# Adding two accumulators of exponentials: by a VectorE instruction, or by an accumulating transfer that GpSimd issues

## The chip, the cores and the metric

One Trainium2 chip; the program runs on one of its cores. The metric is the device time of the whole kernel in microseconds, median over runs. The trace calls the engines PE (TensorE matmul), PEld (TensorE weight load), DVE (VectorE), ACT (ScalarE), POOL (GpSimd) and SP (SyncE, which issues most transfers). Shapes are partitions x elements.

## The reference

Two layers, one after the other. The first is attention with 4 batches, 8 heads, 768 positions and head size 64, in which a query sees the keys that fall into the same of 16 clusters. The second mixes tokens and channels.

```python
def _attn_ref(q, k, v, centroids):
    ...
    mask = q_assign[:, :, :, None] == k_assign[:, :, None, :]
    scores = scale * np.matmul(q, k.transpose(0, 1, 3, 2))
    scores = np.where(mask, scores, -1000000000.0)
    scores = scores - np.max(scores, axis=-1, keepdims=True)
    attn = np.exp(scores)
    attn = attn / (np.sum(attn, axis=-1, keepdims=True) + 1e-09)
    return np.matmul(attn, v).astype(np.float32)

def _moe_ref(x, w_theta, w_tok_r, w_tok_i, w_ch):
    theta = x @ w_theta
    zr, zi = x * np.cos(theta), x * np.sin(theta)
    y = np.einsum('ts,bsd->btd', w_tok_r, zr) + np.einsum('ts,bsd->btd', w_tok_i, zi)
    u = x + y
    return (u + np.maximum(u @ w_ch, 0.0)).astype(np.float32)
```

The change touches the row sums of `attn` alone, the denominator.

## The kernel before

**Pairs, halves, units.** The attention works on 16 pairs of heads (4 batches x 4 pairs; `pi` is the pair, `j` the head in it). The queries of a pair stand in two halves of 384 (`a` = 0, 1), the keys in six blocks of 128 (`i`). A half and a block of keys make a unit, so a pair has 12 units, numbered through (`u` = 12 `pi` + 6 `a` + `i`). The loop goes two units at a time, 192 units in all.

**A unit.** TensorE makes the scores of the key block against the half, transposed, keys on the partitions, once for each head (line 374, tile `sc`). ScalarE takes exp into `at`, a tile of 128 x 768 for both heads (line 437). TensorE multiplies `at` with the values (line 509, `av`). Ten units ahead TensorE also makes the scores with queries on the partitions (line 374, tile `m`), of which VectorE takes the maximum (line 396, `nm`).

**The sums.** The sum over keys is a sum over six units and then over 128 partitions. GpSimd adds the `at` of units 0 to 2 of a half into one accumulator, `acc[a, 0]`, those of units 3 to 5 into another, `acc[a, 1]` (`add_exps`, line 448, two additions each; `TERMS` = 3). `add_sums` then adds the second to the first (line 452). `sums` lets TensorE add over the partitions with a column of ones (line 476, `sm`), one product for each head and half, ScalarE adds a small constant (line 482, `se`), and the sums go out through DRAM, come back spread over partitions, are inverted (line 494, `sq`) and come back broadcast (line 499, `rb`). `normalise` multiplies the pair's output with them (line 530, `xt`; on GpSimd for pairs 0 to 13, on VectorE for the last two) and stores it (line 533). In the last pair `add_sums` isn't called; TensorE adds both accumulators there.

**The order.** It is written out by hand. `at_unit(u, fn, ...)` puts a function on the list of a unit, and the loop takes the lists up as it comes to the units, in order of unit and, on one unit, in the order in which they were put there. At the end of each step `in_order` chains the instructions of each engine, those that issue transfers too, in the order in which they were written. What bears on the change:

```python
        if pi < NPAIR - 1:
            for a in range(2):
                at_unit(7 if pi == a == 0 else u + ADDS[a], add_sums, pi, a)
        stages([u + NU + k for k in SUMS], sums(pi))
        stages([u + NU + k for k in NORM], normalise(pi))
```

This stands in the loop over pairs, with `u` = 12 `pi`, `NU` = 12, `ADDS` = (8, 13), `SUMS` = (4, 6, 8, 9, 10) and `NORM` = (13, 16). So, counted in units from the start of a pair: the first half's accumulators are added at unit 8, the second half's at 13, and TensorE sums over the partitions at 16. On unit 13 also stands `normalise` of the pair before, put on the list one turn of the loop earlier. Within a step the loop writes the scores of unit `u` and `add_exps(u)`, then the lists up to `u`, then scores, exp and `add_exps(u + 1)`, then the list of `u + 1`.

**Buffers.** `acc` has six buffers, taken in turn, four by each pair. `at` has six.

**The rest.** Beside the units GpSimd makes the low parts of queries and keys (line 360), and in the first ten pairs those of weights (line 159). VectorE converts weights from 64-bit floats (lines 137 to 146) and finds the clusters (lines 278 to 286, 339). After the attention comes the second layer (lines 729 to 941), with a first rotation of it (line 550) laid into the last units.

Of the kernel before, what the change touches and what calls it, by code (L numbers as in the profile page):

```python
# [14 lines left out]
ALU = mybir.AluOpType  # L15
# [26 lines left out]
def kernel(  # L42
# [19 lines left out]
    nc = tc.nc  # L62
# [386 lines left out]

    def add_sums(pi, a):  # L450
        s = st[pi]
        nc.vector.tensor_tensor(out=s["acc", a, 0], in0=s["acc", a, 0], in1=s["acc", a, 1], op=ALU.add)  # L452

    def both(products, u, then, *banks):
        interleave(*(products(u, j, *banks) for j in range(2)))
# [213 lines left out]
    for pi in range(NPAIR):  # L669
        u = NU * pi  # L670
        if pi > 0:
            prepare(pi, g1 if pi == 1 else assign(pi))
            at_unit(u - NU + 7, load_v, pi)
        for a in range(2):
            at_unit(u + a * NT - LEAD + NT, shift_row, pi, a)
# [5 lines that stand above are left out]
# [312 lines left out]
```

## Time and profile before

| what | before |
|---|---|
| median of 3 runs | 800.63 us (800.31 to 800.96) |
| span of the profiled execution | 798.5 us, mean granted TensorE clock 0.996 |
| time of the profiled execution itself | not given beside the span |
| DMA | 67.13 MB, mean 84 GB/s |
| transfers issued by GpSimd | none |
| additions of line 452 | 30 (two for each of 15 pairs) |

The profile is one execution, its times counted from the first instruction. A group's row has the line, the engine, the operation, what it writes and reads, and how often; then busy time, the mean of one, and the idle time before it with what ended it. The chain of work that ended last is followed back from the last instruction: at each step to what released it. Matmuls are pipelined and their ends are modelled, so TensorE shown busy need not be at its peak. The attention takes up to about 455 us, the second layer the rest.

### The profile page before, as it was taken

The numbers are of one execution on the slowest core, as the hardware profiler recorded it, in microseconds if no ns is written. First come the engines' busy times: TensorE is split into PE (matmuls) and PEld (weight loads), VectorE is DVE, ScalarE is ACT, GpSimd is POOL, SyncE is SP. The second block draws the span as 40 slices with busy tenths as digits, with TensorE's granted clock in tenths as the row PEclk, the third lists the DMA queues.
The fourth block names the chain that finished last, engine by engine and source line by source line (L and its number), as shares of the span: only waits on it lengthen the run. The fifth ranks groups of instructions, "written<-read, shape, count | busy, mean of one in ns | idle before, by whom it ended". The sixth has DMA issues, their size and how long they took to land.

```text
span 798.5 us, 14338 instructions
## 1 busy us (share of the span) xinstructions
PE 783.2 (98%) x5634; PEld 582.6 (73%) x5634; DVE 555.6 (70%) x664; ACT 399.9 (50%) x801; POOL 491.6 (62%) x284
## 2 busy tenths in 40 slices
PE   6999999999999999999999899999999999999998
PEld 5666656565656666666665588898889988899998
DVE  5789999999999999999888669543234433532322
ACT  3366666766767676666655546432433233504310
POOL 3388888999999999888978324551225112322131
PEclk9899999999999999999999999999999999999999
DMA  3232324332443244433452343003000400020001
GB/s 118 60 97 77 104 77 150 103 130 74 147 132 110 79 134 152 131 111 121 124 185 75 114 135 136 1 36 124 0 1 1 158 1 1 1 80 1 1 21 60
DMA packets 30894, 67.13 MB, mean 84 GB/s; under 512 B 8900, under 2 KB 14636, under 8 KB 30444
## 3 DMA queue, kind: packets, MB, share of 16 engines
q1 hardware_dynamic: 30540, 65.80, 25.1%
q8 instruction: 44, 0.72, 0.4%
q10 hardware_dynamic: 288, 0.43, 0.1%
q14 instruction: 22, 0.18, 0.1%
HBM read 50.79 MB, written 15.32 MB: 83 GB/s over the span
## 4 chain that ended last, share of the span: by engine, by line
PE 91%; DVE 6%; issue 1%; DMA 1%; ACT 1%; SPq 0%; ACTq 0%; DVEq 0%
PE y L862 25%; PE sc L374 24%; PE av L509 15%; PE tp L594 8%; PE cy L885 5%; PE m L374 3%; PE cp L885 3%; PE sm L476 2%; PE lg L263 2%; PE xp L587 1%; DVE nm L396 1%; PE y L885 1%; DVE acc L452 1%; PE lt L275 1%; DVE w L146 1%
## 5 line engine op out<-in xcount | busy, mean ns | idle before, releaser
L437 ACT ACTIVATE at<-sc 128x384 f32<-128x384 f32 x384 | 173.4, 493 | 96.6 <-PE m L374 59.7
L396 DVE TENSOR_REDUCE nm<-m 128x1 f32<-128x768 f32 x192 | 179.6, 945 | 21.4 <-PE m L374 17.1
L448 POOL TENSOR_TENSOR acc<-at,at 128x768 f32<-128x768 f32 x64 | 129.3, 2021 | 36.9 <-ACT at L437 36.5
L374 PE MATMUL m<-hk,hq 64*128 64x384 f32 x384 | 146.9, 387 | 0.9 <-DVE nm L396 0.8
L509 PE MATMUL av<-at,vt 128*64 128x384 f32 x768 | 145.7, 499 | 0.4 <-ACT xt L524 0.2
L816 POOL TENSOR_TENSOR zlc<-ab,zhc 128x512 fp32r<-128x512 f32 x24 | 32.2, 1340 | 177.3 <-ACT zhc L814 177.3
L448 POOL TENSOR_TENSOR acc<-acc,at 128x768 f32<-128x768 f32 x64 | 132.5, 2070 | 10.0 <-ACT at L437 7.9
L374 PE MATMUL m<-mk,mq 64*128 64x384 f32 x384 | 127.9, 337 | 0.8 <-DVE mk L303 0.8
L374 PE MATMUL sc<-hq,hk 64*128 64x384 f32 x384 | 117.7, 390 | 0.5 <-ACT at L437 0.5
L374 PEld LDWEIGHTS sc<-hq,hk 64*128 64x128 f32 x384 | 56.1, 184 | 61.9 <-issue 28.2
L374 PE MATMUL sc<-lq,hk 64*128 64x384 f32 x384 | 98.1, 336 | 0.0
L374 PE MATMUL sc<-mq,mk 64*128 64x384 f32 x384 | 97.8, 334 | 0.0
L374 PE MATMUL sc<-hq,lk 64*128 64x384 f32 x384 | 97.6, 334 | 0.0
L509 PEld LDWEIGHTS av<-at,vt 128*64 128x64 f32 x768 | 46.7, 136 | 59.4 <-issue 53.4
L599 DVE TENSOR_SCALAR kk<-tp 128x512 int32<-128x512 f32 x23 | 15.9, 690 | 95.1 <-PE tp L594 95.1
L374 PEld LDWEIGHTS m<-hk,hq 64*128 64x128 f32 x384 | 70.7, 185 | 3.5 <-DVE nm L396 2.7
L374 PEld LDWEIGHTS m<-mk,mq 64*128 64x128 f32 x384 | 71.4, 187 | 1.0 <-ACT hq L356 1.0
L452 DVE TENSOR_TENSOR acc<-acc,acc 128x768 f32<-128x768 f32 x30 | 70.6, 2352 | 0.0
L876 POOL TENSOR_TENSOR ul<-xT,uh 128x384 fp32r<-128x384 f32 (+1 forms) x36 | 33.8, 962 | 40.6 <-ACT uh L875 35.9
L588 ACT COPY xn<-xp 128x512 f32<-128x512 f32 x23 | 13.5, 586 | 84.2 <-PE xp L587 84.2
L374 PEld LDWEIGHTS sc<-mq,mk 64*128 64x128 f32 x384 | 55.2, 185 | 0.0
L374 PEld LDWEIGHTS sc<-lq,hk 64*128 64x128 f32 x384 | 55.2, 186 | 0.0
(173 smaller groups left out, 1735.5 us busy)
## 6 DMA issues: line engine op xcount, KB each, us to landing
rawq<-in_qT_dram SPq DMA_DIRECT2D x16, 384.0 KB
vt<-in_v_dram SPq DMA_DIRECT2D x16, 384.0 KB
rb<-sd SPq DMA_DIRECT2D x32, 192.0 KB
xT_d<-xt SPq DMA_DIRECT2D x16, 384.0 KB
rawk<-in_kT_dram SPq DMA_DIRECT2D x15, 384.0 KB
w<-in_wrT_dram SPq DMA_DIRECT2D x6, 768.0 KB
w<-in_wiT_dram SPq DMA_DIRECT2D x6, 768.0 KB
xT<-xT_d SPq DMA_DIRECT2D x3, 1536.0 KB
```

What stands on the lines that cost most here:

```text
L263: nc.tensor.matmul(lg[32 * g:32 * g + 32], lhsT=cb[:, p, :, :], rhs=raws[n][:, a * HS:(a + 1) * HS], start=True, stop=True)
L374: nc.tensor.matmul(out, lhsT=stat[r, cols], rhs=mov[r, over], start=start, stop=stop)
L396: nc.vector.tensor_reduce(out=s["nm", a][:, j, i // 2:i // 2 + 1], in_=s["m", j][:, :, 0:HS], op=ALU.max, axis=AX.XY, negate=True)
L437: last_exp[0] = nc.scalar.activation(out=s["at", a, i][:, j], in_=s["sc", j], func=AF.Exp, scale=SCALE)
L448: last_acc[0] = nc.gpsimd.tensor_tensor(out=s["acc", a, x], in0=prev, in1=at, op=ALU.add)
L452: nc.vector.tensor_tensor(out=s["acc", a, 0], in0=s["acc", a, 0], in1=s["acc", a, 1], op=ALU.add)
L509: nc.tensor.matmul(s["av"][64 * j:64 * j + 64], lhsT=s["vt"][:, i, j, :], rhs=s["at", a, i][:, j], start=(i == 0), stop=(i == NT - 1))
L594: nc.tensor.matmul(tp, lhsT=xx[:, c, :], rhs=w_th[c][k], start=(n == 0), stop=(n == 3 * NCT - 1))
L816: nc.gpsimd.tensor_tensor(out=zl, in0=tr, in1=zh.bitcast(F32), op=ALU.subtract)
L862: nc.tensor.matmul(y_at(b, d, c0, c1), lhsT=zz[:, d * P:(d + 1) * P], rhs=ww[:, c0:c1], start=first and lead, stop=last, skip_group_check= ...
L876: nc.gpsimd.tensor_tensor(out=ul[:, d, :], in0=x, in1=uh[:, d, :].bitcast(F32), op=ALU.subtract)
L885: nc.tensor.matmul(cp, lhsT=w_c[d][k][:, e * P:(e + 1) * P], rhs=uu[:, d, :], start=(n == 0), stop=(n == 3 * NCT - 1), skip_group_check=True)
```

## The change

`add_sums` calls GpSimd's transfer instead of VectorE's addition: `acc[a, 1]` is the source, `acc[a, 0]` the destination, both in SBUF, and the DMA engines add the source to what the destination holds. The place on the units' lists is the same.

```diff
     def add_sums(pi, a):
         s = st[pi]
-        nc.vector.tensor_tensor(out=s["acc", a, 0], in0=s["acc", a, 0], in1=s["acc", a, 1], op=ALU.add)
+        nc.gpsimd.dma_start(out=s["acc", a, 0], in_=s["acc", a, 1], accum_op=ALU.add)
```

## The prediction

> **What bounds the kernel now.** I read first the page's busy times and slices, then its chain of work by engine.
>
> ```profile
> span 798.5 us, 14338 instructions
> ...
> PE 783.2 (98%) x5634; PEld 582.6 (73%) x5634; DVE 555.6 (70%) x664; ACT 399.9 (50%) x801; POOL 491.6 (62%) x284
> ...
> PE   6999999999999999999999899999999999999998
> ...
> DVE  5789999999999999999888669543234433532322
> ...
> POOL 3388888999999999888978324551225112322131
> ...
> PE 91%; DVE 6%; issue 1%; DMA 1%; ACT 1%; SPq 0%; ACTq 0%; DVEq 0%
> ```
>
> TensorE carries 91% of the chain, VectorE 6%. In the attention, up to about 455 us, VectorE and GpSimd are nearly as full as TensorE. So an addition taken from VectorE is worth only what of that 6% it causes, and one engine that is almost as full receives something. How evenly TensorE runs there is read from the chain in order of time: the same product, one step of the loop, starts once per pair of heads.
>
> ```profile
> 84.30 1.44 PE av L509 x8
> ...
> 104.02 2.51 DVE acc L452
> ...
> 110.81 1.44 PE av L509 x8
> ...
> 130.52 2.51 DVE acc L452
> ...
> 137.31 1.44 PE av L509 x8
> ...
> 163.27 1.44 PE av L509 x8
> ...
> 262.66 1.44 PE av L509 x8
> ...
> 288.59 1.44 PE av L509 x8
> ...
> 423.28 2.28 DVE acc L452
> ```
>
> A pair takes 26.51 and 26.50 us where the addition stands on the chain (pairs 2 and 3), 25.96 in the next and 25.93 in the middle. The addition is on the chain three times of 30. Everywhere else TensorE paces the pair and VectorE's load is covered by it.
>
> **What goes from VectorE.** The view of line 452, and of two GpSimd lines beside it (ns, least/median/most):
>
> ```profile
> L452 DVE TENSOR_TENSOR acc<-acc,acc x30: 949/2306/2594, 48.3 to 423.3; 128x768 f32<-128x768 f32 x30
> ...
> who waited for it (us, times):
> ...
> L530 POOL TENSOR_TENSOR xt<-xt,rb x14: 1846/2558/2562, 89.0 to 424.7; 128x768 f32<-128x768 f32 x14
> ```
>
> Thirty additions go; the group sums to about 30 x 2.3 = 69 us of VectorE. One took 0.95 us, the median 2.31: most of that is waiting beside GpSimd's own additions. Nobody is listed as waiting for them. Their worth in time: pairs 2 and 3 fall to the 25.96 of pair 4, 2 x 0.54 = 1.1 us. The third place on the chain is the end of the attention:
>
> ```profile
> 437.48 2.08 DMA sq<-sd
> ...
> 439.72 0.64 DVE kk L599
> ...
> 438.27 1.07 PE L594 MATMUL xp_tp<-wth_hi,xl 128*128 128x512 f32 x4
> ```
>
> There VectorE's 2.28 us would move the transfer of sq forward, but the next instruction, kk, also needs the product that ends at 439.34. So kk can move by 0.4 us of the 2.3, and I take 0.4 (ends 0 and 2.3). If TensorE were not the cover in the other pairs, the additions would be worth up to 27 x 0.95 us; the even 25.93 us says it is.
>
> **Where the transfer stands.** One pair in the timeline (start, duration; order of the engines as written):
>
> ```profile
> 259.87 2.59 DVE L452 TENSOR_TENSOR acc<-acc,acc 128x768 f32<-128x768 f32 x1
> ...
> 261.72 2.42 POOL L448 TENSOR_TENSOR acc<-acc,at 128x768 f32<-128x768 f32 x1
> ...
> 270.04 1.83 POOL L448 TENSOR_TENSOR acc<-at,at 128x768 f32<-128x768 f32 x1 [0.42 <-DMA rb<-sd]
> ...
> 270.38 2.31 DVE L452 TENSOR_TENSOR acc<-acc,acc 128x768 f32<-128x768 f32 x1
> ...
> 271.83 2.56 POOL L530 TENSOR_TENSOR xt<-xt,rb 128x768 f32<-128x768 f32 x1
> ...
> 276.55 0.16 PEld L476 LDWEIGHTS sm<-acc,ecol 128*32 128x32 f32 x8 [0.60 <-issue]
> ```
>
> The first half's sum (259.87) is wanted by sm at 276.55, 16.7 us later: any transfer is hidden there. The second half's sum is not so free. VectorE has it ready at 272.69, 3.9 us ahead of sm. GpSimd comes to it late: unit 13's work list holds the multiplication of the pair before (L530) ahead of the sum, and GpSimd issues in that order. So the transfer leaves after unit 13's addition, which ends at 271.87, and after L530, which without VectorE beside it takes 1.85 (its least): 273.72. That leaves **2.8 us** until TensorE reaches sm. Behind sm in TensorE's queue stand the scores and maxima of the next units, so a late sum stops ScalarE and VectorE too; and as TensorE paces the pair, each microsecond late is a microsecond of the kernel, once per pair. VectorE's and SP's queues lose and gain no wait. The six buffers of the accumulators stand it: the buffer that the transfer reads is next written 14 units later for the first half and 15 for the second.
>
> **What the transfer takes.** The profile of before has no transfer issued by GpSimd and none that adds, so I bound it. The nearest rows: a lone store of 384 KB (the same bytes) with the DMA share around it, and the start of the kernel, where two reads of 384 KB run together. The rows of numbers are stretches: from and to, length, busy us of TensorE, its weight loads, VectorE, ScalarE and GpSimd, then clock, DMA share and GB/s.
>
> ```profile
> 410.71 0.33 SPq L156 DMA_DIRECT2D wd5r<-w  x1
> ...
> 410.60:411.40 0.80, 0.80 (x12) 0.60 (x10) 0.80 (x2) 0.80 (x3) 0.34 (x1) 1.00 0.00 0
> 411.40:412.80 1.40, 1.40 (x14) 0.77 (x12) 0.87 (x2) 1.19 (x3) 1.40 (x1) 1.00 0.79 285
> 412.80:414.00 1.20, 1.20 (x10) 0.50 (x7) 1.10 (x2) 0.26 (x1) 1.12 (x2) 1.00 0.00 0
> ...
> 0.72 3.48 DMA rawq<-in_qT_dram
> ...
> rawk<-in_kT_dram ACTq DMA_DIRECT2D x1, 384.0 KB
> ...
> L221 POOL TENSOR_TENSOR cs<-cs,half 128x1 f32<-128x1 f32 x1 | 0.6, 572 | 2.1 <-DVE cs L218 2.1
> ```
>
> - Low end: the store is done by 412.80, 2.1 us after its issue began. It moves the bytes once and SP issued it.
> - Like for like in bytes read: an accumulating transfer reads source and destination, 2 x 384 KB. That is what rawq and rawk read together, and rawq landed 3.48 us after its issue.
> - GpSimd's own time to issue: between SP's 0.33 and a whole pass over the tile, 1.83; its smallest arithmetic instruction took 0.57. I take the middle, 1.08.
>
> My value: 3.48 - 0.33 + 1.08 = **4.2 us**; low end 2.1; high end 1.83 + 3.15 + one more pass of data (3.48 - 2.08, the small transfer above against the large) = 6.4. I take the middle because two reads and a different issuer both lengthen the lone store, and nothing here shows a second pass. The stall is then 4.2 - 2.8 = **1.4 us per pair**, between 0 and 3.6.
>
> The Trainium skill, DMA: Bandwidth & Descriptors, Anatomy of one DMA, gives another sum: for transfers issued from GpSimd about 2.0 us and the bytes at 436 GB/s, an estimate of 2.9 us for these 393,216 bytes, hence a stall of 0.1 and a time near 801. No run here shows such a transfer. Against it the skill's Collectives: The Full Stack, The bandwidth ceiling, says that an adding transfer runs at half the rate of a copying one because it reads two sources; that would add 0.9 us by the same figure, an estimate of 3.8 and a stall of 1.0.
>
> **GpSimd's budget.** In the same pair:
>
> ```profile
> 262.66:288.59 25.93, 25.93 (x216) 15.85 (x218) 24.56 (x25) 17.55 (x38) 25.36 (x13) 1.00 0.36 118
> ```
>
> GpSimd is busy 25.36 of 25.93 us. It gets back what VectorE's additions cost it: L530 goes from 2.56 to 1.85, and the addition at 261.72 from 2.42 to the 1.83 of an undisturbed one, 1.3 us together. It pays two issues, 2.2. New load 26.2, in a pair that the stall makes 27.3 long: it fits, so I add nothing; if it didn't, unit 13 would start late and the difference would add to the stall. The DMA engines are 0.36 busy; two more transfers of some 2.5 us each leave them well below full.
>
> **The last two pairs** have less room:
>
> ```profile
> 401.22 1.85 POOL L530 TENSOR_TENSOR xt<-xt,rb 128x768 f32<-128x768 f32 x1 [1.00 <-DMA rb<-sd]
> ...
> 404.80 0.53 PE L476 MATMUL sm<-acc,ecol 128*32 128x384 f32 x4
> ...
> 422.94 1.81 POOL L448 TENSOR_TENSOR acc<-at,at 128x768 f32<-128x768 f32 x1 [2.00 <-ACT at L437]
> ...
> 427.99 0.85 PE L476 MATMUL sm<-acc,ecol 128*32 128x384 f32 x8
> ```
>
> Pair 13: 404.80 - 403.07 = 1.7, stall 2.5. Pair 14: 427.99 - (424.75 + 1.85) = 1.4, stall 2.8. Pair 0 has no L530 ahead of its sum (L530 runs 14 times on GpSimd, for pairs 1 to 14), so nothing for it.
>
> **Sum.** 12 x 1.4 + 2.5 + 2.8 = 22.1; less 1.1 and 0.4: +20.6 us. The page gives the span, 798.5, 2.1 under the median of 800.63, and no time of the profiled execution itself; I work in differences and add them to the median: **821 us**. With the high end: 12 x 3.6 + 4.7 + 5.0 - 1.5 = +51, 852. With the low end: 0.4 + 0.7 - 1.5 = -0.4, 800.
>
> **Rivals.**
> - *The transfer is hidden (not slower).* It lands within 2.8 us of L530's end; that is the point from which it decides. For it: the lone store took 2.1 us and in these microseconds no large transfer runs. Against: the second read and GpSimd's issue. Time: 800.63 - 1.5 = 799.1 if the last pairs hide too, 800.2 if they don't. The skill's fit named above falls here.
> - *GpSimd becomes the bound (slower).* Its load is 24.1 us and two issues; a pair lasts 25.9 plus the stall, which also grows with one issue. It decides from an issue of about 2.2 us, above my upper bound of 1.83. With 2.5 a pair takes 29.1, 3.2 more, 14 times: 844.
> - *The adding is slow in the DMA engines (slower still).* Landing 8 us after L530: 5.2 per pair, 12 x 5.2 + 13 - 1.5 = +74, 874. No row speaks for it; none excludes it.
>
> **How the numbers follow.** A change of 0.2%, 1.6 us, is about what this kernel's measurement can tell. My forecast (a stall of 0.3 to 3.6 us per pair) 0.62; hidden 0.20; GpSimd bound 0.08; slow adding 0.10. All but the hidden case are slower: 0.80. The hidden case gains 0.4 to 1.5 us, which is just short of 0.2%: same 0.15, faster 0.05 for a tail that gives more than 0.4. The range starts below the hidden case, 799.5, and ends at 848, near the high end; it leaves out most of slow adding and a part of the gainers, under 2 in 10. The forecast's own range is 803 to 852.
>
> **What would show it.** VectorE's busy time near 486 us. Line 452 on GpSimd, 30 issues of about 1.1 us. L530 and the additions behind it near 1.85. Ahead of sm, TensorE idle 1.4 us per pair on a wait for the transfer into acc, and the steps of the middle pairs 27.3 us apart, those of pairs 2 and 3 too. Were the pairs 25.9 us apart, the transfer was hidden; were GpSimd without idle time at unit 13, it is the bound. The prediction fails if GpSimd's issue together with the landing is under 2.8 us or over 6.4.

## The result, and the profile after

The changed kernel takes 913.33 us (median of four runs, 911.14 to 920.16), the kernel before 800.80 beside it: a ratio of 1.1415, 95% interval 1.137 to 1.1459, 112.5 us more. The profiled execution took 911.14 us, its span is 909.3. The page's busy times, three of its rows of slices, the queue of GpSimd's transfers, the chain by engine and the median landing of the transfers:

```profile
span 909.3 us, 14373 instructions
...
PE 831.6 (91%) x5634; PEld 603.0 (66%) x5634; DVE 586.9 (65%) x634; ACT 401.7 (44%) x801; POOL 471.7 (52%) x314
...
PE   7998898798799798798789878999999999999998
...
DVE  5877887888888898887896635685333433343222
...
POOL 3585686686687685675675653265222512241231
...
q0 software_dynamic: 4320, 11.80, 7.3%
...
PE 74%; issue 11%; DVE 9%; DMA 5%; ACT 1%; SPq 1%; POOL 0%; POOLq 0%; ACTq 0%; DVEq 0%
...
acc<-acc POOLq DMA_DIRECT2D x30, 384.0 KB, 4.7
```

GpSimd has less work than before (471.7 us, was 491.6) and gaps in every slice of the attention: it is not the bound. TensorE carries 74% of the chain instead of 91%, and its busy time rose by 48 us for the same 5634 products, so they take longer in the records. VectorE lost thirty additions and yet is busy 31 us longer. The three lines that matter: GpSimd's transfer, a step of the weight conversion on VectorE, and the multiplication that was expected to get faster (ns, least/median/most).

```profile
L452 POOL DMA_DIRECT2D acc<-acc x30: 851/868/1056, 49.4 to 530.5; - x30
...
DMA to landing us min/median/max: 3.9/4.7/6.3
...
L140 DVE TENSOR_SCALAR w<-w x16: 550/8934/9750, 40.2 to 527.3; 128x768 int32<-128x768 int32 x12, 128x512 int32<-128x512 int32 x4
...
L530 POOL TENSOR_TENSOR xt<-xt,rb x14: 1832/1832/2582, 95.1 to 527.9; 128x768 f32<-128x768 f32 x14
```

Before, line 140 read:

```profile
L140 DVE TENSOR_SCALAR w<-w x16: 1177/1305/2066, 40.6 to 427.7; 128x768 int32<-128x768 int32 x12, 128x512 int32<-128x512 int32 x4
```

It is a shift of integers in a tile of weights and has nothing to do with the sums; it stands in VectorE's order near the second half's transfer. What it does there shows in one pair (timeline: start, duration, engine, line, idle time before in brackets):

```profile
231.84 1.83 POOL L530 TENSOR_TENSOR xt<-xt,rb 128x768 f32<-128x768 f32 x1
...
233.62 0.86 POOL L452 DMA_DIRECT2D acc<-acc  x1
...
234.23 2.11 POOL L448 TENSOR_TENSOR acc<-acc,at 128x768 f32<-128x768 f32 x1
...
234.88 8.95 DVE L140 TENSOR_SCALAR w<-w 128x768 int32<-128x768 int32 x1
...
236.03 2.07 POOL L360 TENSOR_TENSOR lq<-rawq,hq 128x768 fp32r<-128x768 f32 x1
...
236.55 0.83 PE L476 MATMUL sm<-acc,ecol 128*32 128x384 f32 x2
237.59 0.85 PE L476 MATMUL sm<-acc,ecol 128*32 128x384 f32 x6 [0.21 <-DMA acc<-acc]
...
237.79 2.10 POOL L448 TENSOR_TENSOR acc<-at,at 128x768 f32<-128x768 f32 x1
...
239.59 2.06 POOL L360 TENSOR_TENSOR lk<-rawk,hk 128x768 fp32r<-128x768 f32 x1
...
241.36 2.04 POOL L448 TENSOR_TENSOR acc<-acc,at 128x768 f32<-128x768 f32 x1
...
243.75 0.95 DVE L396 TENSOR_REDUCE nm<-m 128x1 f32<-128x768 f32 x1
...
244.75 0.68 PE L374 MATMUL m<-hk,hq 64*128 64x384 f32 x1 [4.41 <-DVE nm L396]
...
245.24 0.52 PE L374 MATMUL m<-mk,mq 64*128 64x384 f32 x1
...
246.32 2.83 PE L509 MATMUL av<-at,vt 128*64 128x384 f32 x8
...
251.02 1.84 POOL L448 TENSOR_TENSOR acc<-at,at 128x768 f32<-128x768 f32 x1 [7.62 <-ACT at L437]
```

Behind the transfer GpSimd runs five instructions without a pause, until 241.36 + 2.04 = 243.40. VectorE's shift begins at 234.88 and ends at 243.83, 0.43 us after the last of the five: it got in when GpSimd stopped. The maximum of line 396 stands behind it in VectorE's order, TensorE waits 4.41 us for that maximum, and GpSimd then sits idle 7.62 us, because TensorE's scores and so ScalarE's exponentials are late. Fourteen instructions of VectorE took more than 2.7 us in this run, twelve of line 140 and two of line 143, and none did before. Each stands beside such a row (of two to five instructions) behind a transfer and ends 0.3 to 0.8 us after the row.

The row alone doesn't do it. In the kernel before, GpSimd ran the same five instructions from 274.34 on without a pause, and the shift beside them took 1.30 us:

```profile
274.34 2.14 POOL L448 TENSOR_TENSOR acc<-acc,at 128x768 f32<-128x768 f32 x1
...
275.59 1.30 DVE L140 TENSOR_SCALAR w<-w 128x768 int32<-128x768 int32 x1
...
276.44 2.14 POOL L360 TENSOR_TENSOR lq<-rawq,hq 128x768 fp32r<-128x768 f32 x1
```

The stall costs TensorE a second time. The pair as a stretch, from and to, length, busy us of TensorE, its weight loads, VectorE, ScalarE and GpSimd, then granted clock, DMA share and GB/s; behind it, in a fence of its own, the 4.5 us after the wait:

```profile
216.60:250.80 34.20, 29.59 (x218) 17.30 (x216) 29.23 (x23) 17.53 (x38) 23.64 (x14) 0.90 0.40 112
```

```profile
244.70:249.20 4.50, 4.45 (x17) 2.02 (x17) 3.55 (x4) 1.31 (x2) 0.00 (x0) 0.50 0.20 74
```

The clock is 0.50 after the wait, and the eight products of `av` take 2.83 us where they take 1.51 elsewhere. The Trainium skill, TensorE: Matmul & The Clock Gate, What's actually happening, says that after about 3.4 us without work the array runs at half its pulses until some 3.4 us of work have passed; a wait of 4.4 us followed by 0.50 agrees; the low clock lasted about 5 us here.

The pair is 8.27 us longer than the 25.93 before. TensorE's idle time in it is 34.20 - 29.59 = 4.61: the 4.41 at the maximum and the 0.21 at `sm`. Its busy time is 29.59 - 25.93 = 3.66 longer. About 2.5 of that is the clock (half of the 5 us from 244.7 to where products again take 0.33), and 0.8 is `sm`: its eight products took from 236.55 to 238.44, 1.89 us instead of 0.85, of which 0.21 is the idle time named. There the records show TensorE busy while its weight load waited for the sum. So the late sum that was forecast is in the pair, with 1.0 us beside some 6.9 that weren't (4.4 of waiting and 2.5 of low clock).

Over the kernel (who waited for what: us, times, longest):

```profile
PE m L374 <- DVE nm L396: 48.6, 14, 4.4
...
PE sm L476 <- DMA acc<-acc: 15.2, 14, 4.2
```

### The profile page after: what moved, and what is told of

The parts are those of the page before. It is cut to its first block, busy times and chain, and to the rows that moved or that the text cites. A ratio compares the mean times of both kernels' runs of the same rounds, so it can differ in the third digit from the quotient of the medians.

```text
span 909.3 us, 14373 instructions
## 1 busy us (share of the span) xinstructions
PE 831.6 (91%) x5634; PEld 603.0 (66%) x5634; DVE 586.9 (65%) x634; ACT 401.7 (44%) x801; POOL 471.7 (52%) x314
## 4 chain that ended last, share of the span: by engine, by line
PE 74%; issue 11%; DVE 9%; DMA 5%; ACT 1%; SPq 1%; POOL 0%; POOLq 0%; ACTq 0%; DVEq 0%
PE y L862 22%; PE sc L374 16%; PE av L509 11%; PE tp L594 7%; PE m L374 5%; PE cy L885 4%; DVE nm L396 3%; PE cp L885 2%; DVE w L137 2%; DMA acc<-acc 2%; PE lg L263 2%; DMA sd<-sq 1%; PE xp L587 1%; DVE w L143 1%; PE y L885 1%
## 5 line engine op out<-in xcount | busy, mean ns | idle before, releaser
L374 PE MATMUL m<-hk,hq 64*128 64x384 f32 x384 | 155.8, 410 | 48.6 <-DVE nm L396 48.6
L448 POOL TENSOR_TENSOR acc<-at,at 128x768 f32<-128x768 f32 x64 | 123.6, 1932 | 143.4 <-ACT at L437 141.3
L509 PE MATMUL av<-at,vt 128*64 128x384 f32 x768 | 160.2, 540 | 0.5 <-ACT xt L524 0.2
L448 POOL TENSOR_TENSOR acc<-acc,at 128x768 f32<-128x768 f32 x64 | 124.6, 1947 | 30.9 <-ACT at L437 29.4
L374 PE MATMUL m<-mk,mq 64*128 64x384 f32 x384 | 134.7, 354 | 0.8 <-ACT hq L356 0.8
L374 PEld LDWEIGHTS m<-hk,hq 64*128 64x128 f32 x384 | 76.4, 200 | 53.5 <-DVE nm L396 52.9
L140 DVE TENSOR_SCALAR w<-w 128x768 int32<-128x768 int32 (+1 forms) x16 | 108.1, 6758 | 0.0
L374 PEld LDWEIGHTS sc<-hq,hk 64*128 64x128 f32 x384 | 57.8, 192 | 70.2 <-issue 36.7
L374 PE MATMUL sc<-lq,hk 64*128 64x384 f32 x384 | 103.5, 354 | 0.0
L374 PEld LDWEIGHTS m<-mk,mq 64*128 64x128 f32 x384 | 77.3, 203 | 1.1 <-ACT hq L356 1.1
L374 PEld LDWEIGHTS sc<-hq,lk 64*128 64x128 f32 x384 | 58.1, 196 | 0.0
```

The lines of the kernel that those rows point to most:

```text
L140: nc.vector.tensor_scalar(out=wi, in0=wi, scalar1=5, scalar2=2, op0=ALU.logical_shift_left, op1=ALU.logical_shift_right)
L374: nc.tensor.matmul(out, lhsT=stat[r, cols], rhs=mov[r, over], start=start, stop=stop)
L448: last_acc[0] = nc.gpsimd.tensor_tensor(out=s["acc", a, x], in0=prev, in1=at, op=ALU.add)
L509: nc.tensor.matmul(s["av"][64 * j:64 * j + 64], lhsT=s["vt"][:, i, j, :], rhs=s["at", a, i][:, j], start=(i == 0), stop=(i == NT - 1))
```

## The experiments

Three theories stood against each other. P: once GpSimd has issued a transfer, VectorE's instructions that share a way to SBUF with it get no turn between GpSimd's instructions, as they did before, but only when GpSimd next has nothing to do. The way to SBUF is the theory's name for what is waited for; no view names it. L: the late sum in front of `sm` is the cause, and the rest follows from it. A: the adding in the DMA engines is the cause, or the traffic in SBUF.

**1. The kernel before, with a copy that nobody waits for, issued by GpSimd or by SyncE.** VectorE's addition stays.

```diff
         nc.vector.tensor_tensor(out=s["acc", a, 0], in0=s["acc", a, 0], in1=s["acc", a, 1], op=ALU.add)
+        scr = dram.tile([P, 2, HS], F32, name=f"scr{pi}_{a}")
+        nc.gpsimd.dma_start(out=scr, in_=s["acc", a, 1])      # second kernel: nc.sync
```

> The kernel before with VectorE's additions kept; behind each of the 30, GpSimd also issues a plain transfer of the second accumulator to a scratch in DRAM that nobody reads. Theory P (port): once GpSimd has issued a transfer its next instructions overlap, and VectorE's instructions that share its SBUF port (L140 in the changed kernel: 6.8 us mean against 1.4) get no turn until GpSimd idles; the issue alone is enough. P expects 890 to 950 us, L140 over 5 us in the mean, and VectorE's additions starved too. Theory L (late sum): the 113 us are TensorE's wait for the landed sum at sm and the low clock after it; nobody waits here, so 800 to 805. Theory A (adding): the read-modify-write of SBUF in the DMA engines blocks VectorE; there is none here, so 800 to 805 too.

> The same 30 plain transfers to a scratch in DRAM beside VectorE's additions, issued by SyncE. All three theories expect 799 to 806 us; were it over 820, the transfers' traffic itself, or the reading of the accumulator, would be the cause, and none of the three would stand.

Issued by GpSimd: 906.09 us, ratio 1.1323 (1.1289 to 1.1358). Issued by SyncE: 800.72, ratio 1.0004 (0.9994 to 1.0015). No sum comes later than before and nothing is added in a transfer, and nearly the whole loss is there; the same bytes from SyncE cost nothing. L and A fall as the cause. Line 140 of the first kernel, and its transfer:

```profile
L140 DVE TENSOR_SCALAR w<-w x16: 1178/8667/8668, 39.9 to 530.7; 128x768 int32<-128x768 int32 x12, 128x512 int32<-128x512 int32 x4
```

```profile
L454 POOL DMA_DIRECT2D scr<-acc x30: 557/590/777, 49.0 to 532.5; - x30
```

The part of P's expectation that had VectorE's own additions of line 452 starved as well was wrong: they took 941/2258/2597, as before. They stand ahead of the issue, not behind it.

**2. The same with 512 bytes,** one row, to tell the issue from what it moves.

```diff
+        scr = dram.tile([1, 128], F32, name=f"scr{pi}_{a}")
+        nc.gpsimd.dma_start(out=scr, in_=s["acc", a, 1][0:1, 0, 0:128])
```

> The kernel before with VectorE's additions kept, and behind each GpSimd issues a transfer of one row of 512 bytes to DRAM that nobody reads: as often as in the run with the copy of the whole tile (906 us), with 1/768 of the bytes. P, in the form that the issue leaves GpSimd's cores out of step whatever is sent: 880 to 910 us. If the starving needs the transfer's size (descriptors of 128 rows, or the traffic): 800 to 815.

904.3 us, ratio 1.1301 (1.1282 to 1.1319). The page gives the landing, the timeline the rest:

```profile
scr<-acc POOLq DMA_DIRECT2D x30, 0.5 KB, 2.4
```

```profile
227.22 0.57 POOL L454 DMA_DIRECT2D scr<-acc  x1
...
227.63 0.94 DVE L396 TENSOR_REDUCE nm<-m 128x1 f32<-128x768 f32 x1
...
227.82 1.83 POOL L448 TENSOR_TENSOR acc<-acc,at 128x768 f32<-128x768 f32 x1
...
228.49 8.63 DVE L140 TENSOR_SCALAR w<-w 128x768 int32<-128x768 int32 x1
...
234.91 1.79 POOL L448 TENSOR_TENSOR acc<-acc,at 128x768 f32<-128x768 f32 x1
```

The transfer has landed 2.4 us after its issue, about 229.6; the shift ends at 237.12, 0.42 after GpSimd's last instruction. Neither size nor flight time counts, the issue does. GpSimd's own instructions are at full speed here (1.79 to 1.83), undisturbed by VectorE: the turns that VectorE used to get between them are gone.

**3. The changed kernel, with a handshake behind each transfer:** GpSimd writes one column, VectorE copies it, GpSimd copies that.

```diff
         nc.gpsimd.dma_start(out=s["acc", a, 0], in_=s["acc", a, 1], accum_op=ALU.add)
+        nc.gpsimd.memset(w0, 0.0)
+        nc.vector.tensor_copy(out=w1, in_=w0)
+        nc.gpsimd.tensor_copy(out=w2, in_=w1)
```

> The changed kernel; behind each accumulating transfer GpSimd clears one column, VectorE copies it and GpSimd copies that, so that GpSimd's next instruction starts only when all of GpSimd has ended the one before. P expects that GpSimd's instructions no longer overlap by 0.3 us, that L140 falls to about 1.4 us and TensorE's wait for nm goes, and that the late sum stays: 1 to 2 us in each of 14 pairs and 0.3 us for the round, 812 to 835 us. L expects 905 to 925, since the transfer lands no earlier; A expects 905 to 925 as well.

857.96 us, ratio 1.0735 (1.0683 to 1.0787), above the 812 to 835 expected. Line 140 is back:

```profile
L140 DVE TENSOR_SCALAR w<-w x16: 1167/1298/2179, 40.2 to 485.9; 128x768 int32<-128x768 int32 x12, 128x512 int32<-128x512 int32 x4
```

The largest new wait is the handshake's own:

```profile
DVE rs L455 <- POOL rs L454: 118.6, 30, 6.6
```

VectorE reaches its copy early and stands there for GpSimd, 30 times, up to 6.6 us; the waits at the maximum are down to 18.6 us, and none is listed at `sm` for a transfer. GpSimd now carries 24% of the chain, so at least a part of the loss that remains is another bound, which the handshake brought with it.

**4. The changed kernel, with `drain` behind each transfer,** an instruction that lets GpSimd finish what it has begun; and the same with the sums taken later.

```diff
+        nc.gpsimd.drain()
```

> The changed kernel; GpSimd drains (waits until its own instructions have ended) behind each accumulating transfer, and no other engine has a part in it. P: no overlap of 0.3 us, L140 back to about 1.3 us, no wait of TensorE for nm; what is left is the late sum, 1 to 1.5 us in each of 14 pairs, with part of the low clock behind it: 808 to 828 us. If instead the drain waits for the transfer's landing too (4 us, twice in a pair), GpSimd has 24 + 1.7 + 8 us of work in a pair of 25.9 and becomes the bound: 890 or more. L: 905 to 920, as the sum lands no earlier.

> The same with the drain, and sm two units later. P: both causes are gone; VectorE is freer than before, so pairs 2 and 3 lose their 0.5 us: 798 to 804 us. L: 800 to 806 too. What differs is the step from the kernel with the drain alone: by P and L together it is the price of the late sum, 8 to 25 us.

893.82 us, ratio 1.1151 (1.1115 to 1.1188), and 893.68, ratio 1.1145 (1.11 to 1.1189). In the first, line 140 is at 418/1168/2180, so the starving is gone here too, but `drain` lasts until the transfer has landed:

```profile
228.34 0.87 POOL L452 DMA_DIRECT2D acc<-acc  x1
...
233.72 1.80 POOL L448 TENSOR_TENSOR acc<-acc,at 128x768 f32<-128x768 f32 x1 [4.52 <-issue]
```

In each of the thirty cases GpSimd's next instruction starts 0.24 or 0.25 us after the transfer's landing. Idle times of 3.3 to 5.2 us, 4.2 in the mean, make GpSimd late, and the transfers with it: TensorE's matmuls wait 57.8 us at `sm`. That is the 890 or more that the expectation names for a `drain` that waits. The second kernel's 798 to 804 missed for the same reason. The pair shows that a pause of GpSimd ends the starving; it can't price the late sum.

**5. The changed kernel, with the sums over partitions two units later.**

```diff
-SUMS = (4, 6, 8, 9, 10)
+SUMS = (6, 7, 8, 9, 10)
```

> The changed kernel with the product sm two units (about 4.3 us) later, at unit 18, the rest of the chain of sums where it was. L expects 800 to 806 us: the sum has landed by then. P expects that only the wait at sm goes, 1.0 us or so in each of 14 pairs, and that L140 stays near 7 us: 890 to 912. A expects the same as P.

915.63 us, ratio 1.1454 (1.1417 to 1.149). L's 800 to 806 is refuted, and P's 890 to 912 just exceeded. One wait of 1.3 us for a transfer is left at `sm`'s matmuls; the rest moved:

```profile
PE m L374 <- DVE nm L396: 77.8, 14, 6.7
```

That is 29 us more than after the change alone. TensorE waits for the late maximum in any case, so an earlier wait at `sm` only shortens the later one: in this kernel the late sum costs next to nothing beside the starving.

**6. The second half's transfer alone;** VectorE adds the first half's accumulators.

```diff
+        if a == 1:
             nc.gpsimd.dma_start(out=s["acc", a, 0], in_=s["acc", a, 1], accum_op=ALU.add)
+        else:
+            nc.vector.tensor_tensor(out=s["acc", a, 0], in0=s["acc", a, 0], in1=s["acc", a, 1], op=ALU.add)
```

> Only the second half's sum (unit 13) by the transfer; the first half's (unit 8) by VectorE as before. P: the row of five instructions stands behind this transfer, so nearly the whole loss stays: 885 to 915 us. L: the same, as only the second half's sum is late.

910.6 us, ratio 1.1356 (1.1301 to 1.1411). The transfer at unit 13, with the row of five behind it, carries the loss; beside it, the one at unit 8 adds nothing that shows.

**7. Other places for the transfers.** If the starving lasts until GpSimd's next pause, a transfer just ahead of a pause should be harmless.

```diff
-ADDS = (8, 13)
+ADDS = (6, 12)     # second kernel (8, 12), third (12, 12)
```

> The changed kernel with the transfers at units 6 and 12 of a pair, not 8 and 13: each then stands in GpSimd's order ahead of an addition that waits for ScalarE's next exp. P: where GpSimd idles behind the issue, VectorE gets its turns again, and the second sum leaves 4 us earlier, so it isn't late either; unit 12 has such a gap in every pair, unit 6 only where GpSimd has caught up. 798 to 806 if both gaps hold, up to 830 if unit 6 finds none. L: the sum is early, so 798 to 806. A (the adding blocks VectorE): 890 or more.

> The changed kernel with the second half's transfer at unit 12, the first half's still at 8. P: the row of five instructions no longer stands behind an issue without a gap, so most of the loss goes; what L339 and L284 lose behind unit 8's issue stays: 800 to 825. L: 798 to 806.

> Both transfers at unit 12, ahead of the one gap that the kernel before has in every pair (unit 13's addition waits for ScalarE). The gap must hold two issues, 1.7 us; both land some 6 us after, about when TensorE comes to sm. P: 798 to 815, depending on whether anything of the gap is left; if nothing is left, starved as in the changed kernel, 890 or more. L: 800 to 815.

819.23 us, ratio 1.0232 (1.0217 to 1.0247); 821.62, ratio 1.0255 (1.0239 to 1.0271); and 802.1, ratio 1.0019 (0.9998 to 1.0039). In the first two, three pairs each still have VectorE starved, now at line 137 (up to 9.6 and 11.5 us), with five and four waits at the maximum; here is the first kernel's row:

```profile
PE m L374 <- DVE nm L396: 14.7, 5, 4.7
```

The expectation that unit 12 has a gap in every pair failed in just these three: GpSimd's next addition follows the issue at once, as in the first kernel here.

```profile
162.84 0.86 POOL L452 DMA_DIRECT2D acc<-acc  x1 [0.30 <-POOL acc L448]
...
163.44 2.12 POOL L448 TENSOR_TENSOR acc<-at,at 128x768 f32<-128x768 f32 x1
...
165.24 9.60 DVE L137 TENSOR_SCALAR w<-w 128x768 f32<-128x768 f32 x1
```

In the third, GpSimd pauses behind the second issue of every pair (0.22 us in the same pair is enough), and line 140 is at 1189/1322/2086. Its page:

```profile
span 798.9 us, 14373 instructions
...
PE 783.0 (98%) x5634; PEld 582.3 (73%) x5634; DVE 520.7 (65%) x634; ACT 400.5 (50%) x801; POOL 495.8 (62%) x314
```

All thirty transfers are there, VectorE has 35 us less to do than before the change (555.6), and the time is that of before. Of all that was run this is the best version of the change, and it gains nothing.

**8. The weight conversion four units later,** away from the transfer, in the changed kernel (also with the sums later) and in the kernel before.

```diff
-    W_UNITS = (8, 11.5, 14, 15, 16, 18, 19.5)
+    W_UNITS = (12, 15.5, 18, 19, 20, 22, 23.5)
```

> The changed kernel with the preparation of the weights (load, L135 to L146, the low part) four units later, so that VectorE's L137 to L146 fall on units 6 to 10 of a pair, where GpSimd idles between its additions, and not on units 2 to 6, where it has five instructions in a row behind the second transfer. P: L140 finds idle GpSimd within some 2 us; most of the loss goes: 815 to 860 us. L: no change, 905 to 920.

> The changed kernel with the weights' preparation four units later and sm two units later. If the late sum is what stays (20 us of waits at sm in 14 pairs, and the low clock behind them): 798 to 808 us, with no wait of TensorE for the transfer. If VectorE is still starved somewhere and sm only shows it: 820 or more.

> The kernel before (additions on VectorE) with the preparation of the weights four units later, as in the run at 838 us. If the move costs nothing, 799 to 803 us, and the 36 us are the transfer's; if VectorE or the end of the attention suffers from it, 805 to 838, and that much of the 36 is the move's.

838.21 us, ratio 1.0468 (1.0423 to 1.0513); 834.08, ratio 1.0383 (1.0349 to 1.0418); and 836.73, ratio 1.0423 (1.0398 to 1.0449). In the first, line 140 is at 560/1686/1918, no instruction of VectorE takes over 2.7 us, and the wait at `sm` is still there:

```profile
PE sm L476 <- DMA acc<-acc: 20.0, 14, 4.7
```

The move itself costs 34 us in the kernel before, as the third kernel shows. The first and the third come out 1.5 us apart, but they aren't bound by the same thing. Here are the chains by engine, the first kernel's and the third's:

```profile
PE 77%; DMA 8%; issue 6%; ACT 3%; POOL 3%; DVE 2%; POOLq 0%; DVEq 0%; ACTq 0%
```

```profile
PE 81%; DVE 16%; issue 1%; ACT 1%; DMA 0%; DVEq 0%; ACTq 0%
```

In the third, VectorE's instructions stand back to back on the chain. In the first, VectorE is relieved of the additions and nearly off it, and the 8% are the landing of the transfer at `sm`, pair after pair: with the starving gone, the late sum that was forecast binds the kernel. So the near equality says nothing about the rest of the 112 us. Nor is the loss here the late sum's price in the changed kernel, for the low part of the weights (line 159), moved too, now stands close ahead of the second half's transfer in GpSimd's order.

In the second no wait for a transfer is left at `sm`, but VectorE is starved again, at line 137:

```profile
L137 DVE TENSOR_SCALAR w<-w x16: 547/5644/6520, 38.9 to 466.5; 128x768 f32<-128x768 f32 x12, 128x512 f32<-128x512 f32 x4
```

That is the 820 or more of its expectation.

## Why the prediction was wrong

The sign was right and the place, unit 13, too; the size and the cause were not. The forecast was 821 us with a range up to 848.

- **What goes from VectorE: right.** The additions were worth next to nothing; with no starving and no late sum (`ADDS` = (12, 12)) the time is 802.1 against 800.75.
- **The transfer: nearly right.** GpSimd's issue took 0.87 us (taken: 1.08, bounds 0.33 and 1.83), the landing 4.7 us median, 3.9 to 6.3 (taken 4.2, bounds 2.1 and 6.4). The fit of the Trainium skill (DMA: Bandwidth & Descriptors, Anatomy of one DMA), an estimate of 2.9, is below every landing of the change; the copy of experiment 1 landed in 2.6 us at least and 3.6 in the median. The time that the prediction gives for that fit, near 801, is a slip: with the last two pairs' stalls of 1.2 and 1.5 us its own sum comes to 803.
- **L530 ahead of it: right,** it fell to 1.83 (taken 1.85).
- **The stall at `sm`: about right.** 15.2 us in 14 pairs on TensorE's matmuls, 24.9 on its weight loads, against 22.1. But it is not what the time is made of, as experiment 5 shows; only where nothing is starved does it bind (the first kernel of 8).
- **GpSimd's budget: right that it fits,** though the sum was 2.6 us high (23.64 us busy in a pair, 26.2 forecast). It counts GpSimd's own time alone and so couldn't show what VectorE loses. The rival in which GpSimd is the bound is out: 52% busy over the kernel.
- **"VectorE's and SP's queues lose and gain no wait": the step that failed.** In the list of waits it holds: VectorE has none there for GpSimd. But the shift behind the issue took 8.9 us instead of 1.3 once it had begun, its queue with it, and TensorE with the maximum in that queue. The profile of before had the ground for the doubt: the additions of line 452 at 2.31 us against 0.95, stretched beside GpSimd. I read that as a cost per instruction that would go away, and didn't ask what lets VectorE in between two GpSimd instructions, or what an issue does to that.
- **Rivals.** The hidden transfer was not it, nor the slow adding. None of the three held this mechanism, and the range's upper end was built from the transfer's duration alone.

The Trainium skill has the neighbour of it. SBUF — State Buffer, Who interferes with whom, says that VectorE and GpSimd share one pair of ports, which a `tensor_scalar` like line 140 can take, that whoever issues first holds it for the whole instruction and that the other blocks until then. By that an instruction of VectorE waits for one of GpSimd's: 1.83 + the 0.43 us that it took once GpSimd had stopped, an estimate of 2.26, and before the change line 140 indeed never took more than 2.07. After an issue it waited through five, 8.95 us; the measurement decides, the rule is too short there.

**What stays open.** Why an issue has this effect. GpSimd's successive instructions overlap by some 0.3 us behind an adding transfer (234.23 + 2.11 against 236.03), as if parts of the engine were out of step and one of them always at the port. The Trainium skill, GPSIMD Engine Reference, §2.1 Instruction dispatch, says that its cores begin an instruction each as soon as they are through with the one before, which would allow that, and a handshake or a pause ended the starving. But behind the plain copies the overlap is about 0.05 us, as in the kernel before (274.34 + 2.14 against 276.44), and the starving the same, so this is a guess. No run put a short GpSimd instruction of another kind in the issue's place, so it isn't shown that only an issue does this. Open too is the late sum's own price in time: wherever it was removed, another bound stood (5, the second kernel of 8 and the second of 4).

## What to carry to other kernels

When a transfer is moved to GpSimd, look for what GpSimd does behind the issue: if it runs on without a pause, instructions of VectorE like those of lines 137, 140 and 143 wait for the end of that row, not for one instruction, and whoever follows in VectorE's order waits too. Issue the transfer just ahead of a pause of GpSimd, or from another queue; SyncE's plain copy cost nothing here, but no run had SyncE issue an adding one. And before any of this, ask what the relief of an engine is worth that the pacing engine already covers: here nothing, even at the best place.

## What the runs showed of the hardware

- From GpSimd's issue of a transfer until GpSimd next pauses, a VectorE shift of 128x768 didn't get in: 8.6 to 8.9 us in the median instead of 1.3, with 384 KB added, 384 KB copied or 512 bytes copied alike; SyncE's copy of 384 KB had no such effect. Lines 137 and 143 were held up in the same way, for up to 11.5 and 9.0 us.
- Not all of VectorE's instructions are concerned: the maximum of line 396 kept its 0.94 us right behind an issue and beside GpSimd's addition (227.63 in experiment 2).
- An adding transfer of 384 KB within SBUF: 0.87 us of GpSimd, landing after 4.7 us; a plain copy of it to DRAM 0.59 and 3.6; 512 bytes 0.57 and 2.4.
- `drain` on GpSimd behind a transfer waits for its landing: 3.3 to 5.2 us of idle time, ending 0.24 us after it.
- After a wait of 4.4 us TensorE's granted clock was 0.50 for about 5 us.
